# Batch 1's queries: from 32 half-width transposes of the loaded tile to 16 full ones of a copy repacked by GpSimd

## The chip, the cores and the metric

The kernel runs on one core of one Trainium2 chip. The metric is the device time of one execution in microseconds. The kernel before took 283.73 us, the median of six runs from 283.51 to 283.94.

## The reference

The program is a linear attention followed by a two-layer perceptron. `q`, `k` and `v` have shape 8 batches x 8 heads x 576 rows x 64.

```python
kv  = einsum('bhsd,bhse->bhde', k, v)      # 64 x 64 for each batch and head
out = einsum('bhsd,bhde->bhse', q, kv)
out = out / sqrt(mean(out * out, -1) + 1e-6) * g_norm
x   = out.transpose(0, 2, 1, 3).reshape(4608, 512)
h   = x @ w_in                             # 512 -> 2048
g   = where(h > 0, h, exp(min(h, 0)) - 1)
return g @ w_out                           # 2048 -> 512
```

The products run in bf16 with fp32 sums.

## The kernel before, in words

The 4608 rows are worked in nine tiles T. Tiles 0 to 7 are rows 0 to 511 of each batch (four groups j of 128 rows, `J = 4`, `G = 512`); tile 8 gathers the remaining 64 rows of every batch. Each tile passes through these stages:

1. the kv product of a batch (`kv_single`, L174): 64x64 matmuls of k and v into the PSUM buffer `at`, which ScalarE copies to `kv_sb` (L352);
2. the queries are turned, so that the 64 head dimensions lie on partitions (two heads to 128 partitions), into the tile `qT`;
3. the scores (L373 for tile 1, L201 later), then squares, sums over heads, reciprocal root and row scale, and a transpose into `xT`;
4. the first product `mm1` (L467), the elu (L479 to L498), and the second product `mm2` (L514), whose result ScalarE copies out (L527).

The order on every engine is written out by hand: the program runs under a manual schedule, each engine takes its instructions in the order in which the code issues them, and pieces of the attention of tile T + 1 are placed between the matmuls of tile T. `mm2_quarter(0, j, i)` is four matmuls of 128x512: row group j and weight slabs 4i to 4i+3 of tile 0's second product. The first eight pieces of that product are where the change is: quarter 0 for j = 0 to 3, then quarter 1 for j = 0 to 3.

Three ways of turning queries exist. Tile 0 has its own at the start. Tile 1, which the change touches, uses TensorE: `q_t` calls `q_t_single` (L185) for each of four head pairs, into a tile from the pool `ps_at`, which has one buffer of two PSUM banks. This tile is called `at` in the profile; kv products and some scores use the same one buffer. Two ScalarE copies (L249, L250) then move it to `qT`. Tiles from 2 on are repacked on GpSimd (`unpack_q`, four copies at L150) and turned by a transposing DMA (L256).

GpSimd's queue (POOL) holds nearly all loads, which also cast from fp32 to bf16. At most eight of them are under way: a load waits until the one eight places ahead of it has landed. For the stretch around the change the order is: k and v of batch 1, a small copy of batch 0's kv (L770), the weight slabs of `w_out` 10 to 12, 12 to 14 and 14 to 16 (L142), then q, k and v of batch 2. The queries of batch 1 were issued before, at 13.67 and 15.07 us, one transfer for each half of the heads, and lie in the tile `q_pk` as 128 rows x head x j x 64.

The code that sets the order around the change, before it:

```python
    load_w_out(10, 12)
    load_w_out(12, 14)
    ...
    for j in range(J):
        mm2_quarter(0, j, 0)
        if j == 2:
            at["q"]()
    for j in range(J):
        mm2_quarter(0, j, 1)
        if j == 1:
            at["kvu0"]()
        if j == 2:
            at["seu0"](scores)
```

`at["q"]` is `q_t` of tile 1, `at["kvu0"]` the kv product of its first half of head pairs, `at["seu0"]` the scores of that half.

Of the kernel before, what the change touches and what calls it, by code (L numbers as in the profile page):

```python
# [16 lines left out]
def kernel(  # L17
# [13 lines left out]
    nc = tc.nc  # L31
    P = 128
# [5 lines left out]
    J = 4  # L38
# [18 lines left out]
    ident = const.tile([P, P], BF16, name="ident")  # L57
# [13 lines left out]
    raw, bf = {}, {}  # L71
# [52 lines left out]
    def after(ap):  # L124
        nc.gpsimd.tensor_copy(out=gate, in_=ap)  # L125

    def unpack_q(b, eng):
        t = raw.pop(("q", b))
        bf["q", b] = qkvp.tile([P, J, H, D], BF16, name="q_bf", tag="q")
        for j in range(J):  # L130
            if j == J - 1:
                after(bf["v", b][0:1, 0, 0, 0:1])
            copy_on(eng, bf["q", b][:, j], t[:, :, j])

# [5 lines left out]
    def load_w_out(f0, f1):  # L140
        fs = slice(f0, f1)
        nc.gpsimd.dma_start(  # L142
            out=w_out_sb[:, fs, :], in_=moe_w_out.rearrange("(c p) f -> p c f", p=P)[:, fs, :]
        )

    def copy_on(eng, out_, in_):
        if eng is nc.scalar:
            nc.scalar.copy(out_, in_)
        else:
            eng.tensor_copy(out=out_, in_=in_)  # L150
# [13 lines left out]
    def at_tile(dtype):  # L164
        full = ps_at.tile([P, 1024], FP32, name="at", tag="at")
        return full if dtype == FP32 else full.bitcast(BF16)
# [12 lines left out]
                        stop=(j == RK - 1),  # L179
                    )  # L180

    def q_t_single(q_pk, qt_ps, r, p):
        for j in range(J):
            for l in range(2):
                nc.tensor.transpose(  # L185
                    qt_ps[l * 64 : l * 64 + 64, r, j * P : j * P + P],
                    q_pk[:, 2 * p + l, j, :],
                    ident,
                )

    def se_mm(T, h, qT, banks):

# [47 lines left out]
    def attention(T):  # L240
        st = {}

        def q_t():
            qt_ps = at_tile(BF16).rearrange("p (r t) -> p r t", r=NPAIR)
            qT = attp.tile([P, NPAIR, G], BF16, name="qT", tag="qT")
            st["qT"] = lambda p, j: qT[:, p, j * P : j * P + P]
            for p in range(NPAIR):
                q_t_single(raw["q", T], qt_ps, p, p)
            nc.scalar.copy(qT[:, 0:2, :], qt_ps[:, 0:2, :])  # L249
            nc.scalar.copy(qT[:, 2:4, :], qt_ps[:, 2:4, :])  # L250

# [152 lines left out]
        def x_u(u, eng):  # L404
# [21 lines left out]
            return turn  # L426

        pieces = {"kv": kv_all, "q": q_t, "qd": q_dma, "se": se}
        pieces["landed"] = lambda: after(st["at"])
        for h in range(2):  # L430
# [78 lines left out]
    def mm2(T, j, f0, f1, hold=False):  # L509

        if f0 == 0 and (T, j) not in o_ps:
            o_ps[T, j] = ps_m2.tile([P, DM], FP32, name="o_ps", tag="mm2")
        for f in range(f0, f1):
            nc.tensor.matmul(  # L514
                o_ps[T, j],
                lhsT=gT[T][:, f, j * P : j * P + P],
                rhs=w_out_sb[:, f, :],
                start=(f == 0),
                stop=(f == FC - 1),
            )  # L520
        if f1 == FC and not hold:
            mm2_out(T, j)
# [8 lines left out]
    def mm2_quarter(T, j, i):  # L531
        mm2(T, j, 4 * i, 4 * i + 4)
# [18 lines left out]
    V, A, Q = nc.vector, nc.scalar, nc.gpsimd  # L551
# [72 lines left out]
    def turned(n):  # L624
        return bank(n).bitcast(BF16).rearrange("p (r t) -> p r t", r=2)
# [3 lines left out]
    qt_ps = turned(3)  # L629
# [137 lines left out]
    at, ahead = attention(1), attention(2)  # L767
# [3 lines left out]
        out=kv_sb[:, 0].rearrange("p (s u) e -> p u s e", s=2), in_=kv0  # L771
    )
    load_w_out(10, 12)
    load_w_out(12, 14)
    load_w_out(14, FC)
    fetch_packed_q(2)
# [6 lines left out]
    scores = ps_m1.tile([P, 2, G], FP32, name="se_ps", tag="mm1")  # L783
    for j in range(J):
        mm2_quarter(0, j, 0)
        if j == 2:
            at["q"]()
    for j in range(J):
        mm2_quarter(0, j, 1)
        if j == 1:  # L790
            at["kvu0"]()
        if j == 2:
            at["seu0"](scores)
            at["sq0"]()
            at["sum0"]()
# [9 lines left out]
    for j in range(J):  # L805
        mm2(0, j, 10, 12)
        if j == 1:
            at["inv1"]()
            at["xu0"](scores[:, 0, :])
    at["mulu1"]()  # L810
    unpack_q(2, Q)
    ahead["qd"]()
    for j in range(J):
# [8 lines left out]
    def fetch(b):  # L822
        if b < B:
            fetch_packed_q(b)
            packed_kv(b)
            for name in "kv":
                fetch_packed_kv(name, b)
            unpack_q(b, Q)
        else:
            fetch_q(B)  # L830
            cast_q(B, Q)
# [46 lines left out]
    at, ahead = ahead, attention(3)  # L878
# [22 lines left out]
    for T in range(2, NT):  # L901
        at = ahead if T + 1 < NT else None
# [62 lines left out]
```

## Time and profile before

| | |
|---|---|
| median of 6 runs | 283.73 us (283.51 to 283.94) |
| the profiled execution | 283.93 us, span 282.2 us |
| TensorE busy | 273.2 us, 97% of the span |
| VectorE, ScalarE, GpSimd busy | 159.7, 153.7, 55.9 us |
| granted TensorE clock | 1.00 |
| L185, the 32 transposes | one after the other from 31.36 us, 1.01 us in all |
| L150, GpSimd's copies for tiles 2 to 7 | 24, 609 ns median |

The profile names instructions by line, engine, operation and tile. PE is TensorE's matmul, PEld its weight load, ACT ScalarE, DVE VectorE, POOL GpSimd. Times in the timeline are microseconds from the span's start, and in brackets stands how long the engine was idle before an instruction and what ended that. The span is shorter than the execution's own time by 1.7 us, which lies around it. Some matmul records are missing from the trace, so that counts there can be one or two short (x11 for 12).

### The profile page before, as it was taken

To read this page: it belongs to the slowest core of one execution; us is meant where nothing else is said; L and a number is where in the kernel's file an instruction comes from. 1 tells how busy PE (TensorE), PEld (TensorE's weight loads), DVE (VectorE), ACT (ScalarE), POOL (GpSimd) and SP (SyncE) were. 2 spreads that over 40 slices of the span, in tenths; PEclk is the share of its full clock that TensorE was granted. 3 is DMA by queue.
4 is the path that set the end of the run, shared out by engine and by line. 5 is a ranking of instruction groups with operands and counts; after the bars stand their busy time and mean duration, and the time that the engine had idled before them with its cause. 6 is when DMAs were issued, how large, how long until landed. Compare 5 with 4: busy or idle time off the path is not lost.

```text
span 282.2 us, 5133 instructions
## 1 busy us (share of the span) xinstructions
PE 273.2 (97%) x2104; PEld 129.1 (46%) x2134; DVE 159.7 (57%) x232; ACT 153.7 (54%) x221; POOL 55.9 (20%) x98
## 2 busy tenths in 40 slices
PE   7899999999999999999999999999999999999994
PEld 3434454445444444444444444444444444444444
DVE  2549443878388647843693468445854586444400
ACT  2769546666487438533863377237923692333311
POOL 7944422143421241005100421012000000000000
PEclk9999999999999999999999999999999999999999
DMA  7999999697796695358935795455236123010122
GB/s 196 199 200 202 208 201 191 145 196 136 173 194 102 153 177 139 74 149 118 203 76 146 95 216 69 127 115 150 53 95 77 77 38 112 0 77 0 74 76 74
DMA packets 57579, 35.98 MB, mean 128 GB/s; under 512 B 32852, under 2 KB 55124, under 8 KB 57556
## 3 DMA queue, kind: packets, MB, share of 16 engines
q0 software_dynamic: 21808, 17.30, 40.6%
q1 hardware_dynamic: 35348, 17.83, 25.3%
q10 hardware_dynamic: 400, 0.52, 0.5%
q8 instruction: 16, 0.26, 0.4%
q14 instruction: 7, 0.06, 0.1%
HBM read 36.70 MB, written 9.44 MB: 164 GB/s over the span
## 4 chain that ended last, share of the span: by engine, by line
PE 90%; DMA 5%; ACT 1%; issue 1%; DVE 1%; POOL 1%; POOLq 0%
PE h_ps L467 40%; PE o_ps L514 38%; PE o_ps L924 5%; DMA w_in_sb<-in_moe_w_in_dram 3%; DMA k_pk<-in_k_dram 2%; PE at L174 2%; PE at L467 1%; PE at L201 1%; PE bank L684 1%; POOL w_in_sb L136 1%; PE se_ps L201 1%; DVE xs L229 0%; DVE ss L218 0%; ACT elu_e L479 0%; PE at L185 0%
## 5 line engine op out<-in xcount | busy, mean ns | idle before, releaser
L467 PE MATMUL h_ps<-xT,w_in_sb 128*128 128x512 bf16 x532 | 125.5, 379 | 0.2
L514 PE MATMUL o_ps<-w_out_sb,gT 128*128 128x512 bf16 x488 | 118.1, 379 | 1.5 <-issue 0.5
L479 ACT ACTIVATE elu_e<-h_ps 128x1024 bf16<-128x1024 f32 (+1 forms) x71 | 69.9, 995 | 80.8 <-PE h_ps L467 78.5
L467 PEld LDWEIGHTS <-w_in_sb 128*128 128x128 bf16 x552 | 52.5, 98 | 63.2 <-DVE xT L333 1.7
L514 PEld LDWEIGHTS <-gT 128*128 128x128 bf16 x512 | 49.4, 98 | 58.4
L490 DVE TENSOR_SCALAR elu_e<-elu_e 128x1024 bf16<-128x1024 bf16 (+1 forms) x75 | 32.1, 428 | 73.8 <-ACT elu_e L479 73.8
L498 DVE TENSOR_TENSOR gT<-elu_e,h_ps 128x1024 bf16<-128x1024 bf16 (+1 forms) x51 | 60.1, 1179 | 5.3
L527 ACT COPY o_sb<-o_ps 128x512 f32<-128x512 f32 x32 | 18.6, 585 | 15.6 <-PE o_ps L514 15.6
L218 DVE TENSOR_REDUCE ss<-sq 128x16 f32<-128x1024 bf16 x16 | 19.4, 1219 | 11.2 <-ACT sq L213 10.5
L485 ACT ACTIVATE elu_h<-h_ps 128x1024 bf16<-128x1024 f32 (+1 forms) x20 | 19.6, 991 | 0.0
L150 POOL COPY q_bf<-q_pk 128x512 bf16<-128x512 bf16 x24 | 14.4, 629 | 22.9 <-DMA q_pk<-in_q_dram 22.9
L498 DVE TENSOR_TENSOR gT<-elu_e,elu_h 128x1024 bf16<-128x1024 bf16 x20 | 13.8, 692 | 2.6 <-ACT elu_h L485 1.2
L924 PE MATMUL o_ps<-w_out_sb,gT 128*128 128x512 bf16 (+1 forms) x79 | 14.0, 336 | 0.1
L125 POOL COPY gate<-qT 1x1 bf16<-1x1 bf16 x6 | 1.1, 180 | 61.9 <-DMA qT<-q_bf 61.9
L104 POOL DMA_DIRECT2D q_pk<-in_q_dram x14 | 10.5, 757 | 4.3 <-issue 1.5
L229 DVE TENSOR_TENSOR xs<-at,ss 128x512 bf16<-128x512 f32 x16 | 10.2, 681 | 1.2 <-ACT ss L225 1.2
L924 PEld LDWEIGHTS <-gT 128*128 128x128 bf16 x80 | 7.7, 98 | 6.4 <-DVE gT L498 0.4
L213 ACT ACTIVATE sq<-at 128x1024 bf16<-128x1024 f32 x9 | 9.4, 1044 | 1.6 <-PE at L201 1.0
L118 POOL DMA_DIRECT2D k_pk<-in_k_dram x12 | 8.3, 695 | 2.9 <-DMA w_in_sb<-in_moe_w_in_dram 1.2
L118 POOL DMA_DIRECT2D v_pk<-in_v_dram x12 | 8.3, 688 | 3.3 <-DMA w_out_sb<-in_moe_w_out_dram 1.8
L174 PEld LDWEIGHTS <-k_pk 64*64 64x64 bf16 x576 | 6.4, 107 | 4.5 <-issue 4.4
L932 ACT COPY o_last<-o_ps 128x512 f32<-128x512 f32 (+1 forms) x5 | 2.5, 500 | 10.8 <-PE o_ps L924 10.8
(79 smaller groups left out, 138.8 us busy)
## 6 DMA issues: line engine op xcount, KB each, us to landing
out_dram<-o_sb SPq DMA_DIRECT2D x16, 512.0 KB, 3.3
q_pk<-in_q_dram POOLq DMA_DIRECT2D x14, 256.0 KB, 5.4
k_pk<-in_k_dram POOLq DMA_DIRECT2D x6, 576.0 KB, 8.0
v_pk<-in_v_dram POOLq DMA_DIRECT2D x6, 576.0 KB, 10.8
w_in_sb<-in_moe_w_in_dram POOLq DMA_DIRECT2D x5, 256.0 KB, 8.4
st_q<-in_q_dram SPq DMA_DIRECT2D x2, 512.0 KB, 4.7
w_out_sb<-in_moe_w_out_dram POOLq DMA_DIRECT2D x2, 512.0 KB, 13.5
w_out_sb<-in_moe_w_out_dram POOLq DMA_DIRECT2D x4, 256.0 KB, 12.1
```

The costliest lines, as they stand in the source:

```text
L118: nc.gpsimd.dma_start(out=raw[name, b].rearrange("p h j d -> p h (j d)")[:, hs], in_=in_[:, hs])
L150: eng.tensor_copy(out=out_, in_=in_)
L174: nc.tensor.matmul(kv_ps[l * 64 : l * 64 + 64, s, u * 64 : u * 64 + 64], lhsT=bf["k", T][rows, j, 2 * u + l, :], rhs=bf["v", T][rows, j, 2 ...
L218: nc.vector.reduce_sum(out=ss, in_=sq.rearrange("p c (h e) -> p (c h) e", h=H), axis=AX.X)
L467: nc.tensor.matmul(h_ps[a][:, cs], lhsT=w_in_sb[:, c, f * P : f * P + P], rhs=x(c, cs), start=(c == 0), stop=(c == KC - 1),)
L479: nc.scalar.activation(e[:, lo:hi, :], ps, AF.Exp)
L485: nc.scalar.activation(h[:, lo:hi, :], ps, AF.Relu)
L490: nc.vector.tensor_scalar(out=e[:, lo:hi, :], in0=e[:, lo:hi, :], scalar1=1.0, scalar2=1.0, op0=ALU.min, op1=ALU.subtract,)
L498: nc.vector.tensor_tensor(out=gT[T][:, 2 * i + lo : 2 * i + hi, :], in0=e[:, lo:hi, :], in1=h, op=ALU.add if relu else ALU.max,)
L514: nc.tensor.matmul(o_ps[T, j], lhsT=gT[T][:, f, j * P : j * P + P], rhs=w_out_sb[:, f, :], start=(f == 0), stop=(f == FC - 1),)
L527: nc.scalar.copy(o_sb[T][:, j % 2, :], o_ps.pop((T, j)))
L924: nc.tensor.matmul(ps, lhsT=gT[B][:, f, j * P : j * P + P], rhs=w_out_sb[:, f, cols], start=(f == 0), stop=(f == FC - 1),)
```

## The change

Batch 1 gets the repacking that the later batches have. `unpack_q` gets a flag: for the later batches a tiny gating copy stands ahead of the last of its four copies, and for batch 1 it is left out. Its four GpSimd copies, each 128x512 bf16, are issued between the loads of slabs 10 to 12 and 12 to 14; they write the tile `q_bf` as 128 rows x j x head x 64. There two heads lie side by side, so that `q_t_single` takes 128 columns at once: 16 transposes of 128x128 in place of 32 of 128x64 in two halves. The call of `at["q"]` moves from behind quarter 0, j = 2, to behind quarter 1, j = 0: eight matmuls later. The two ScalarE copies, the buffer `at` and all that follows keep their order.

```diff
-    def unpack_q(b, eng):
+    def unpack_q(b, eng, gated=True):
         t = raw.pop(("q", b))
         bf["q", b] = qkvp.tile([P, J, H, D], BF16, name="q_bf", tag="q")
         for j in range(J):
-            if j == J - 1:
+            if gated and j == J - 1:
                 after(bf["v", b][0:1, 0, 0, 0:1])
             copy_on(eng, bf["q", b][:, j], t[:, :, j])
...
-    def q_t_single(q_pk, qt_ps, r, p):
+    def q_t_single(qb, qt_ps, p):
         for j in range(J):
-            for l in range(2):
-                nc.tensor.transpose(
-                    qt_ps[l * 64 : l * 64 + 64, r, j * P : j * P + P],
-                    q_pk[:, 2 * p + l, j, :],
-                    ident,
-                )
+            nc.tensor.transpose(
+                qt_ps[:, p, j * P : j * P + P],
+                qb[:, j, 2 * p : 2 * p + 2, :].rearrange("p h d -> p (h d)"),
+                ident,
+            )
...
-                q_t_single(raw["q", T], qt_ps, p, p)
+                q_t_single(bf["q", T], qt_ps, p)
...
     load_w_out(10, 12)
+    unpack_q(1, Q, gated=False)
     load_w_out(12, 14)
...
     for j in range(J):
         mm2_quarter(0, j, 0)
-        if j == 2:
-            at["q"]()
     for j in range(J):
         mm2_quarter(0, j, 1)
+        if j == 0:
+            at["q"]()
         if j == 1:
             at["kvu0"]()
```

## The prediction

> **What bounds the kernel now.** I read the page first, then the waits of TensorE, then the chain of waits in order of time, and last the timeline of all engines around the edited place. The page's first part settles the engine:
>
> ```profile
> PE 273.2 (97%) x2104; PEld 129.1 (46%) x2134; DVE 159.7 (57%) x232; ACT 153.7 (54%) x221; POOL 55.9 (20%) x98
> ```
>
> TensorE (PE) works 273.2 of 282.2 us. What lies off TensorE is free as long as TensorE does not wait for it. The waits of TensorE, all five that are listed:
>
> ```profile
> PE bank L603 <- DVE zeros L579: 1.5, 1, 1.5
> PE kv_ps L174 <- DMA v_pk<-in_v_dram: 0.7, 2, 0.5
> PE o_ps L514 <- issue: 0.5, 3, 0.2
> PE bank L684 <- DMA w_in_sb<-in_moe_w_in_dram: 0.5, 1, 0.5
> PE bank L666 <- ACT sq L663: 0.4, 2, 0.2
> ```
>
> Four of them belong to the start (lines 603, 684, 666 and the first kv product). After that only 0.5 us of "issue" is listed, and no wait for another engine or a DMA. So after about 20 us TensorE is a gapless queue: time taken off it is gained, time put into it as a stall is lost, and there is no later wait that could swallow a delay. Now the edited place in the chain (start us, us, what):
>
> ```profile
> 31.36 1.01 PE at L185 x32
> 32.38 0.16 issue
> 32.54 2.54 PE o_ps L514 x11
> 35.07 0.41 PE at L174 x36
> ...
> 41.31 0.45 PE se_ps L413 x8
> ```
>
> and the same place in the timeline of all engines (start us, us, engine, instruction, in brackets the idle time before it and who ended it):
>
> ```profile
> 29.02 0.70 POOL L142 DMA_DIRECT2D w_out_sb<-in_moe_w_out_dram x1 [0.61 <-DMA q_pk<-in_q_dram]
> ...
> 31.29 1.08 PE L185 MATMUL at<-ident,q_pk 128*64 128x128 bf16 x32
> 31.51 0.71 POOL L142 DMA_DIRECT2D w_out_sb<-in_moe_w_out_dram x1 [1.80 <-DMA w_out_sb<-in_moe_w_out_dram]
> ...
> 32.42 1.01 ACT L249 COPY qT<-at 128x1024 bf16<-128x1024 bf16 x1 [1.67 <-PE at L185]
> ...
> 32.96 0.74 POOL L104 DMA_DIRECT2D q_pk<-in_q_dram x1 [0.74 <-DMA k_pk<-in_k_dram]
> 33.33 1.02 ACT L250 COPY qT<-at 128x1024 bf16<-128x1024 bf16 x1
> ...
> 35.00 0.48 PE L174 MATMUL at<-v_pk,k_pk 64*64 64x64 bf16 x36
> ```
>
> What to see: the pool `at` has one buffer. The transposes of L185 fill it, ScalarE (ACT) empties it in two copies that start 0.91 us apart and end at 33.33 + 1.02 = 34.35, and the next user of the same buffer is the kv product of L174, at 35.00. The slack between "emptied" and "wanted again" is **0.65 us**. It is made by the 12 big matmuls that stand between L185 and L174 (11 of them recorded), 2.5 us.
>
> **What the Trainium skill says.** (1) "TensorE: Matmul & The Clock Gate", section "Wait — 56ns, not 53.3ns?": 55.6 ns from start to start for 128 columns and 215.7 ns for 512. The trace agrees: eight full 128x128 transposes of L413 take 0.45 us, 56 ns each; eight matmuls of L467 take 1.73 us, 216 ns each. (2) "TensorEngine Tiling (Array Packing)", "Column Tiling" and "Key Properties": with a stationary side of 64 columns two tiles work side by side, and a change of tiling mode drains the engine. The trace agrees: 32 half transposes take 1.01 us, 31.6 ns each, little more than half of 56, and behind them the chain has 0.16 us of "issue"; behind the full transposes of L413 it has none. (3) "GPSIMD Engine Reference", "Key points": GpSimd shares its SBUF interfaces with VectorE. In the trace 24 copies of L150 took 602 to 880 ns, median 609; so contention is there, but seldom. (4) The first page again, "What's actually happening": TensorE's clock is cut after an idle window of about 3.4 us. The trace has the clock at full speed throughout, and nothing in it shows so long a gap in mid-run; the stall I expect is about a third of that.
>
> **The change, part by part.**
>
> *TensorE work.* Removed: 32 half transposes, 1.01 us, and probably the 0.16 us drain behind them. Added: 16 full ones, 16 x 56 ns = 0.90 us. Sum: -0.11 to -0.27 us; I take -0.27, since no drain follows L413. That is 0.1% of the kernel, so the headline edit is almost nothing by itself: half-width transposes were already running in pairs.
>
> *GpSimd queue.* Added behind the weight load of slabs 10 to 12 (issued at 27.70): four copies. The first needs the second half of q_pk, whose arrival releases the queue at 29.02 in the timeline. Four at the 0.576 us pitch of the later groups (three in 1.73 us) end at 29.02 + 2.3 = 31.3; at the slowest copy seen, 880 ns, at 32.5. Passed by them in this queue: the load of slabs 12 to 14 moves from 29.02 to about 31.4, that of 14 to 16 from 31.51 to about 32.1; the two q_pk fetches and k_pk, v_pk of batch 2 keep their times, because the first of them waits until 32.96 for an older k transfer anyway. The moved loads cost nothing, I estimate: a transfer issued in this stretch lands 12.1 us later (29.02 gives 41.1), the transfers before it land some 1.3 us apart in issue order (38.5, 39.8, 41.1 from issue plus time to landing), so its bytes start to move only near 39.8, long after 31.4. If that cover were gone it would land at 31.4 + 12.1 = 43.5, against a first use near 42.6 + 1 us of the shift below: no wait to speak of even then.
>
> *VectorE.* Nothing is added; its elu operations at 28.97 to 31.5 could be slowed by the copies, but what they write (the last slabs of gT) is read at 44 us.
>
> *The move of the transposes.* They go eight matmuls later: 8 x 216 ns = 1.73, from 31.36 to **33.09**. Their input is there (31.3; 32.5 at worst). They end at 33.09 + 0.90 = 33.99. ScalarE's first copy started 0.05 us after all of L185 had ended (32.37, then 32.42), though the engine had been idle for 1.67 us and half of the transposes was done at about 31.9; so it waits for the whole set. In the changed program too only the first copy carries a wait for TensorE. Hence first copy 34.04, second 34.95, end 35.97.
>
> *The new wait.* TensorE, after the transposes, has only the four matmuls of one block, 0.86 us, before the kv product: it is there at 33.99 + 0.86 = 34.85, and `at` is free at 35.97. With 0.08 us from the end of a ScalarE copy to the weight load that it releases (L352 ends 39.85, L373's load starts 39.93), the product starts at **36.05** instead of 35.07 or 35.00: a stall of 1.2 us. Net of the 0.27 us saved and the rest of the order unchanged, everything from the product on is later by 36.05 - 35.00 = **1.05 us**. Behind the stalled product queue all later matmuls, since TensorE keeps their order. ScalarE's kv copy, the scores, squares, sums and row scales hang on the product and shift along with it; their distances to TensorE's later work stay as they were. Transfers get 1.05 us more slack.
>
> *Sum.* +1.05 us on the profiled execution: 283.93 becomes 284.98 (span 282.2 to 283.25). That execution lies 0.20 us above the median of the six runs, 283.73; so I predict **284.8 us**.
>
> *Bounds of the unknown.* Below: if the first copy could start at half of the transposes (33.59), the second would start at 34.50, end at 35.52, and the shift be 0.6. Another 0.1 could be swallowed at 40.34, where four matmuls took 0.97 us instead of 0.86, perhaps waiting for slabs 10 to 12. Above: +0.16 if a drain remains somewhere before the copies, +0.2 for a slower release: about 1.4. I take 1.05, because every term has a row.
>
> **The rivals.**
>
> - *No stall counts* (not slower): ScalarE's drain is overlapped or the shift is absorbed, and only the 0.27 us of TensorE work remains: 283.73 - 0.27 = 283.46 us. Place: the first matmul of the kv product. It decides if `at` is empty by 34.85. For it: ScalarE is idle just before (1.67 us at 32.42), so it copies at once. Against: both copies together need 1.93 us after the last transpose, and TensorE has 0.86 us of work there.
> - *Half-early drain*: the copies chase the transposes, shift 0.5 to 0.6, 284.3 us, at the edge of what counts. Against: the start at 32.42 after 1.67 us idle.
> - *GpSimd late* (slower still): the copies slip behind 33.09, by a late q_pk or contention with VectorE. It decides once four copies take over 4.1 us from 29.02, 1.0 us each; the slowest seen is 0.88. At 1.25 us each they end at 34.0: +0.9 more, 285.7 us.
> - *The full-width form is slower than I think*, drain included, at the price of separate 128-column matmuls: no, L413 shows 56 ns in this very kernel.
>
> **How the numbers follow.** Stall as computed, 84%; half-early 6%, GpSimd late 4%, no stall 6%. About 0.2% (0.57 us) is what a measurement of this kernel can tell from no change. Slower by more: 84 + 4 and a part of the half-early case: 0.88. Within: 0.09. Faster by more: 0.03, for what I don't see, since the TensorE work removed is worth less than 0.57 us. The range, 284.2 to 285.3 us, takes the main case with its bounds (0.6 to 1.4 above 283.73 gives 284.3 to 285.1) and a little for the median's own scatter.
>
> **What would show it.** In the profile after: the 16 transposes at about 33.1, 0.9 us long, with no wait for GpSimd; four copies on POOL from 29.0 to 31.3; the load of slabs 12 to 14 at 31.4; the two ScalarE copies at 34.0 and 34.95; and a new row in TensorE's waits, the kv product behind the copy into qT, about 1.2 us, once. I am wrong if that row is missing, if TensorE waits for q_bf, or if a wait for w_out appears near 42 to 45 us.

## The result, and the profile after

The changed kernel took **284.61 us**, the median of 19 runs (284.26 to 285.33), beside 283.8 us for the kernel before on the same chips. The ratio is 1.003 with a 95% interval of 1.002 to 1.0039, so the change costs 0.6 to 1.1 us: slower, by a little. The prediction was 284.8, from 284.2 to 285.3.

The page of the profile after, TensorE's row:

```profile
PE 272.9 (96%) x2088; PEld 129.3 (46%) x2118; DVE 159.7 (56%) x232; ACT 153.8 (54%) x221; POOL 59.2 (21%) x102
```

TensorE works 0.3 us less than before, in 16 matmuls less, and the span is nevertheless longer, 283.5 us in place of 282.2. The four longest waits of TensorE (us in total, times, longest) say why:

```profile
PE bank L602 <- DVE zeros L578: 1.5, 1, 1.5
PE kv_ps L174 <- DMA v_pk<-in_v_dram: 1.2, 2, 1.0
PE at L174 <- ACT qT L249: 1.2, 1, 1.2
PE o_ps L513 <- issue: 0.5, 3, 0.2
```

The third row is new, and there is one of it: the kv product of batch 1 behind the second ScalarE copy. The second row, 1.2 in place of 0.7, lies in the first microseconds, which neither edit touches: the loads at the start fall a little differently in every execution. In this one the second product of tile 0 began at 28.92 us, before at 28.61. I therefore compare two distances in which that start cancels: **d**, from the first matmul of that product to the first one of batch 1's kv product, and **R**, from the same matmul to the end of the span.

The timeline of the changed kernel at the edited place (line numbers from 184 up to the edited calls near the end are one lower than before):

```profile
28.91 2.60 POOL L150 COPY q_bf<-q_pk 128x512 bf16<-128x512 bf16 x4 [0.39 <-DMA q_pk<-in_q_dram]
28.92 4.48 PE L513 MATMUL o_ps<-w_out_sb,gT 128*128 128x512 bf16 x19
...
30.42 0.62 DVE L489 TENSOR_SCALAR elu_e<-elu_e 128x1024 bf16<-128x1024 bf16 x1
31.14 0.91 DVE L497 TENSOR_TENSOR gT<-elu_e,elu_h 128x1024 bf16<-128x1024 bf16 x1
31.46 1.40 POOL L142 DMA_DIRECT2D w_out_sb<-in_moe_w_out_dram x2
...
33.24 1.06 PE L184 MATMUL at<-ident,q_bf 128*128 128x128 bf16 x16
...
34.33 1.01 ACT L248 COPY qT<-at 128x1024 bf16<-128x1024 bf16 x1 [3.27 <-PE at L184]
...
35.24 1.02 ACT L249 COPY qT<-at 128x1024 bf16<-128x1024 bf16 x1
36.06 0.74 POOL L118 DMA_DIRECT2D k_pk<-in_k_dram x1 [0.77 <-DMA w_out_sb<-in_moe_w_out_dram]
36.31 0.48 PE L174 MATMUL at<-v_pk,k_pk 64*64 64x64 bf16 x36 [1.15 <-ACT qT L249]
```

Read it from the bottom. The kv product sat idle for 1.15 us and started 0.05 us after the second copy into qT had ended (35.24 + 1.02 = 36.26). The first copy began 1.09 us after the first transpose, where before it was 1.13, but now only four matmuls, not twelve, lie between the transposes and the product. Before the change the product of batch 1 began at 35.00, and the second product of tile 0 here:

```profile
28.61 2.75 PE L514 MATMUL o_ps<-w_out_sb,gT 128*128 128x512 bf16 x12
```

So d is 36.31 - 28.92 = 7.39 us, before 35.00 - 28.61 = 6.39: **+1.00 us**. R is 283.5 - 28.92 = 254.6, before 282.2 - 28.61 = 253.6: **+1.0 us**. Nothing of the stall was won back later. The remaining 0.3 us by which the two spans differ is the start.

### The profile page after: what moved, and what is told of

It reads as the page before. It is cut to its first block, busy times and chain, and to the rows that moved or that the text cites. A ratio compares the mean times of both kernels' runs of the same rounds, so it can differ in the third digit from the quotient of the medians.

```text
span 283.5 us, 5104 instructions
## 1 busy us (share of the span) xinstructions
PE 272.9 (96%) x2088; PEld 129.3 (46%) x2118; DVE 159.7 (56%) x232; ACT 153.8 (54%) x221; POOL 59.2 (21%) x102
## 4 chain that ended last, share of the span: by engine, by line
PE 89%; DMA 5%; ACT 2%; issue 1%; DVE 1%; POOL 1%; POOLq 0%
PE h_ps L466 40%; PE o_ps L513 37%; PE o_ps L924 5%; DMA w_in_sb<-in_moe_w_in_dram 3%; DMA v_pk<-in_v_dram 2%; PE at L174 2%; PE at L466 1%; PE at L200 1%; PE bank L683 1%; PE se_ps L200 1%; DVE xs L228 0%; DVE ss L217 0%; ACT elu_e L478 0%; ACT qT L248 0%; ACT sq L212 0%
## 5 line engine op out<-in xcount | busy, mean ns | idle before, releaser
L150 POOL COPY q_bf<-q_pk 128x512 bf16<-128x512 bf16 x28 | 17.5, 658 | 22.2 <-DMA q_pk<-in_q_dram 22.2
L932 ACT COPY o_last<-o_ps 128x512 f32<-128x512 f32 (+1 forms) x5 | 2.5, 501 | 10.8 <-PE o_ps L924 10.8
```

## The experiments

My theory, "one buffer": the loss is the read-out of the one-buffer tile `at`, which the move brought too close to the next user of that buffer. The main rival, "repacking": GpSimd's copies, the loads that they push back, or the full-width form cost the time. All times are medians beside runs of the kernel before on the same chip; d, R and the stall are read from one profiled execution of each kernel.

| kernel | d, us | R, us | stall, us | median, us | ratio to before (95%) |
|---|---|---|---|---|---|
| before | 6.39 | 253.6 | none | 283.7 to 283.9 | |
| the change | 7.39 | 254.6 | 1.15 | 284.61 | 1.003 (1.002 to 1.0039) |
| e1_old_place | 6.17 | 253.3 | none | 283.58 | 0.9996 (0.9988 to 1.0005) |
| e2_move_only | 7.51 | 254.6 | 1.05 | 284.83 | 1.004 (1.0027 to 1.0052) |
| e3_half_way | 6.52 | 253.6 | 0.29 | 284.08 | 1.001 (1.0 to 1.002) |
| e4_later | 8.26 | 256.9 | 2.02 | 287.01 | 1.0107 (1.0087 to 1.0128) |
| e5_dve_drain | 6.79 | 254.3 | 0.56 | 284.63 | 1.0026 (1.0014 to 1.0038) |
| e6_copies_only | 6.40 | 253.5 | none | 283.89 | 1.0008 (0.9995 to 1.0022) |
| e7_filled | 8.25 | 255.4 | 0.50 beside 1.5 of filling | 285.32 | 1.0057 (1.0044 to 1.007) |
| e8_later_dve | 7.66 | 255.2 | 1.43 | 285.42 | 1.0057 (1.0043 to 1.007) |

### The repacking without the move: e1_old_place

```diff
     for j in range(J):
         mm2_quarter(0, j, 0)
+        if j == 2:
+            at["q"]()
     for j in range(J):
         mm2_quarter(0, j, 1)
-        if j == 0:
-            at["q"]()
```

> The changed program, but the transposes stay where they were before the change (behind quarter 0, j = 2). Measure beside the time: d, from the first matmul of tile 0's second product to the first one of the kv product (6.39 us before, 7.39 us after the change). Theory 'one buffer' (the stall is the read-out of the single buffer at, which the move put too close to the kv product): the copies into qT end about 0.5 us before the buffer is wanted again, no stall, d = 6.2 to 6.4 (at most 0.2 of waiting for GpSimd's last copy), time 0 to 0.25 us under before, about 283.6. Rival 'repacking' (GpSimd's copies, the moved loads or the full-width form carry the cost): the time stays near that of the change, some 284.6 to 284.8.

Its timeline around the transposes:

```profile
28.56 2.52 POOL L150 COPY q_bf<-q_pk 128x512 bf16<-128x512 bf16 x4 [0.38 <-DMA q_pk<-in_q_dram]
...
31.08 1.06 PE L184 MATMUL at<-ident,q_bf 128*128 128x128 bf16 x16
...
33.08 1.02 ACT L249 COPY qT<-at 128x1024 bf16<-128x1024 bf16 x1
...
34.66 0.48 PE L174 MATMUL at<-v_pk,k_pk 64*64 64x64 bf16 x36
```

The last copy on GpSimd ends at 31.08 and the transposes begin at 31.08, without a listed wait: just in time in this execution. The buffer is empty at 34.10, 0.56 us before it is wanted. d is 6.17, 0.22 us under before, and R about 0.3 under. So with the move taken back the loss is gone, and what the repacking is worth by itself shows in the profile: about a quarter of a microsecond. The timing (0.9988 to 1.0005) cannot tell this from nothing. No other version has a median below that of the kernel before beside it.

### The move without the repacking: e2_move_only

```diff
     for j in range(J):
         mm2_quarter(0, j, 0)
-        if j == 2:
-            at["q"]()
     for j in range(J):
         mm2_quarter(0, j, 1)
+        if j == 0:
+            at["q"]()
```

This is applied to the kernel before.

> The program before with one edit: the 32 half-width transposes of the loaded tile are issued eight matmuls later, where the change has its 16. No repacking. Theory 'one buffer': the whole loss is here, and a little more since the half-width form is 0.2 us slower: d = 7.5, stall 1.0 to 1.2 us, time about 1.1 us over before, 284.9. Rival 'repacking': no loss, 283.8.

The row in TensorE's waits comes with the move alone:

```profile
PE at L174 <- ACT qT L250: 1.1, 1, 1.1
```

d is 7.51 and the median 284.83: the whole loss, without an added copy on GpSimd. "Repacking" is out.

This run also shows what the half-width transposes cost, since all four matmuls behind them are recorded:

```profile
33.07 1.08 PE L185 MATMUL at<-ident,q_pk 128*64 128x128 bf16 x32
34.09 1.04 PE L514 MATMUL o_ps<-w_out_sb,gT 128*128 128x512 bf16 x4
```

The 20 matmuls of 216 ns from 28.66 on (19 recorded) reach to 32.98, so the block of transposes takes 34.09 - 32.98 = 1.11 us of TensorE. The full-width block of the change takes 34.13 - 33.24 = 0.89. The difference, 0.22, is what e1_old_place gained in d. From the first start to the last the two forms are nearly alike, 0.86 and 0.84 us (1.08 and 1.06 less the 0.22 us that one transpose lasts). The saving is nearly all idle time at the two ends of the half-width block, of which 0.09 us lies ahead of it (32.98 to 33.07).

### Half way, and later: e3_half_way and e4_later

The edits are like that of e1_old_place, with the call behind quarter 0, j = 3, and behind quarter 1, j = 1, ahead of the kv product.

> The changed program with the transposes four matmuls earlier than in the change (behind quarter 0, j = 3), so half way between the two places. Theory 'one buffer': the buffer is free 0.86 us earlier than in the change, d = 6.5, a stall of about 0.3 us, time 0.1 to 0.2 us over before, 283.9. A rival in which the stall does not go with the distance (a fixed cost of the new form) says 284.6 to 284.8.

> The changed program with the transposes four matmuls later still (behind quarter 1, j = 1, straight ahead of the kv product). Theory 'one buffer': nothing of the read-out is covered any more, stall 2.0 us, d = 8.25, time about 1.85 us over before, 285.6. Fixed-cost rival: 284.6 to 284.8.

The wait and the two ends of d, first e3_half_way, then e4_later:

```profile
PE at L174 <- ACT qT L249: 0.3, 1, 0.3
28.07 3.62 PE L513 MATMUL o_ps<-w_out_sb,gT 128*128 128x512 bf16 x15
...
34.59 0.48 PE L174 MATMUL at<-v_pk,k_pk 64*64 64x64 bf16 x36 [0.29 <-ACT qT L249]
```

```profile
PE at L174 <- ACT qT L249: 2.0, 1, 2.0
28.36 5.34 PE L513 MATMUL o_ps<-w_out_sb,gT 128*128 128x512 bf16 x23
...
36.62 0.48 PE L174 MATMUL at<-v_pk,k_pk 64*64 64x64 bf16 x36 [2.02 <-ACT qT L249]
```

From e3_half_way over the change to e4_later each step of four matmuls (0.86 us) lengthens d by 0.87, from 6.52 to 7.39 to 8.26. A fixed cost of the new form is excluded. The times of e3_half_way agree (1.001, 1.0 to 1.002). Those of e4_later do not: 287.0 where I expected 285.6, and R is 3.3 us over before where d explains 1.9. Its page has a dip in the row of the granted clock, and the table by stretches of time (PE, PEld, DVE, ACT, POOL busy us and instructions, then the clock, the DMA share and GB/s) shows where:

```profile
PEclk9999979999999999999999999999999999999999
```

```profile
35.00:37.00 2.00, 0.38 (x36) 0.36 (x35) 0.00 (x0) 1.56 (x2) 1.06 (x2) 1.00 1.21 205
37.00:39.00 2.00, 1.84 (x33) 0.95 (x23) 0.00 (x0) 0.62 (x2) 0.74 (x1) 0.74 1.24 209
39.00:41.00 2.00, 2.00 (x6) 0.70 (x5) 1.22 (x1) 0.71 (x2) 0.00 (x0) 0.50 1.28 199
41.00:43.00 2.00, 1.84 (x42) 0.83 (x41) 1.29 (x2) 0.75 (x3) 0.00 (x0) 0.90 1.44 197
```

After the gap TensorE ran at half clock for 3.41 us: stretches of 0.02 us put the fall at 37.98 and the rise at 41.39. What is missing from full clock in the last three rows is 2 x (0.26 + 0.50 + 0.10) = 1.7 us. Of the five executions four have a mean clock of 0.994 and took 286.73 to 287.17 us; the fifth had 1.000 and took 285.53, what the stall alone predicts.

### A faster read-out: e5_dve_drain

```diff
-            nc.scalar.copy(qT[:, 0:2, :], qt_ps[:, 0:2, :])
-            nc.scalar.copy(qT[:, 2:4, :], qt_ps[:, 2:4, :])
+            nc.vector.tensor_copy(out=qT[:, 0:2, :], in_=qt_ps[:, 0:2, :])
+            nc.vector.tensor_copy(out=qT[:, 2:4, :], in_=qt_ps[:, 2:4, :])
```

> The changed program, but both copies of the turned queries into qT run on VectorE, which has nothing to do from 32 to 39 us, instead of ScalarE. Theory 'one buffer': a VectorE pass over 128x1024 bf16 of PSUM takes 0.75 us in the profile (L422) against 1.01 on ScalarE, so the buffer is free about 0.5 us earlier, d = 6.9 (7.39 in the change, 6.39 before), the stall falls from 1.15 to about 0.65 us, time about 0.5 us over before, 284.3. If TensorE waited for something else there (landing of k or v, a drain), d would stay at 7.39 and the time at 284.7.

Its timeline:

```profile
33.39 0.69 DVE L248 COPY qT<-at 128x1024 bf16<-128x1024 bf16 x1 [2.01 <-PE at L184]
33.99 0.68 DVE L249 COPY qT<-at 128x1024 bf16<-128x1024 bf16 x1
34.77 0.48 PE L174 MATMUL at<-v_pk,k_pk 64*64 64x64 bf16 x36 [0.56 <-issue]
```

With the place unchanged and only the read-out faster, d falls by 0.60 to 6.79, and the product again starts 0.10 us after the second copy. The stall follows the read-out. (A version in which the product has a buffer of its own was not run.) The time follows less well: R is 0.7 over before, where d accounts for 0.4. One new row of 0.2 us, TensorE waiting for a gT of VectorE in the last tile, is part of that: VectorE begins this gT 0.45 us after its preceding operation has ended, 0.10 in the change. Why, stays open. The expected 284.3 lies within the interval (1.0014 to 1.0038 of 283.71 is 284.1 to 284.8), but the measured median does not separate this version from the change.

### GpSimd's part by itself: e6_copies_only

```diff
     load_w_out(10, 12)
+    unpack_q(1, Q, gated=False)
     load_w_out(12, 14)
```

In the kernel before, with the flag that `unpack_q` then needs; the copies' result is not read.

> The program before with GpSimd's four copies of batch 1's queries added at the place where the change has them; what they write is not read, TensorE goes on turning the loaded tile. The copies push the loads of w_out slabs 12 to 14 and 14 to 16 back as in the change. Theory 'one buffer': GpSimd's part is free, d = 6.39, no new wait, 283.8 as before, and slabs 12 to 14 land within 0.3 us of where they landed before. Rival 'repacking': part of the 0.8 us shows here, 284.2 or more.

d is 6.40, R 253.5, TensorE has no new wait. The ratio, 1.0008, does not exclude a few tenths (0.9995 to 1.0022); the profile shows none. The two elu operations of VectorE at the end of the copies took 0.71 and 0.91 us here, so the slowing comes with the added copies. The loads of slabs 12 to 14 and 14 to 16 went out together at 30.93 and landed after 10.0 us (the median of the two), where in the kernel before they took 12.1 and 10.8: they wait in the queue of transfers instead of on GpSimd.

### What the gap does to the clock: e7_filled and e8_later_dve

e7_filled is e4_later with filling in the gap, e8_later_dve is e4_later with the copies of e5_dve_drain.

```diff
             at["q"]()
+            for f in range(7):
+                nc.tensor.matmul(
+                    scores[:, 0, :],
+                    lhsT=gT[0][:, f, 0:P],
+                    rhs=w_out_sb[:, f, :],
+                    start=True,
+                    stop=True,
+                )
```

> The program of e4_later with seven extra 128x512 matmuls between the transposes and the kv product; what they write is overwritten by the scores. They fill the stall of 2.0 us with 1.5 us of work (7 x 216 ns) and so move nothing by themselves: the kv product still waits for the second copy. Theory 'the gap of 2 us cuts the clock' (e4_later showed half clock from about 37 to 41 us in its profile and a mean clock of 0.994 in four of five executions, while the fifth, at 1.000, took 285.53): the clock stays at 1.000, d = 8.25 as there, time 285.5. Rival 'the late place itself costs 3 us' (another wait behind it): 287.0 as in e4_later, whatever the gap is filled with.

> The program of e4_later (transposes straight ahead of the kv product) with both copies into qT on VectorE. The read-out takes 0.6 us less, as e5_dve_drain showed, so the stall is 1.4 us in place of 2.0, d = 7.65. Theory 'one buffer': 1.25 us over before, 285.0, if the clock holds. For the clock it shows a gap between the 1.15 us of the change (never cut) and the 2.0 us of e4_later (cut in four of five): a mean clock of 0.994 and some 286.5 us in part of the executions would say that 1.4 us is already enough.

The table by stretches of e7_filled, two stretches:

```profile
35.00:37.00 2.00, 1.50 (x42) 0.80 (x41) 0.00 (x0) 1.41 (x3) 0.90 (x2) 1.00 1.21 205
37.00:39.00 2.00, 2.00 (x25) 0.89 (x23) 0.00 (x0) 0.97 (x2) 0.58 (x1) 1.00 1.24 207
```

Seven matmuls whose result is not used make e4_later 1.7 us faster (285.32 against 287.01). The kv product starts at the same distance, d = 8.25, and the clock stays at full speed, with means of 0.998 to 1.000 in five executions. So some 1.5 to 1.7 us of e4_later's loss was the clock, and the gap was its cause. In e8_later_dve, with a gap of 1.43 us, none of five executions shows the drop (0.998 to 1.000). Its median, 285.42, is 0.4 over what I expected; like e5_dve_drain it has the 0.2 us wait for gT in the last tile, which stays open.

## Why the prediction was right

- **TensorE's work**, -0.27 us: right in kind, a little large: -0.22 in d of e1_old_place, about -0.3 in R. What was mis-sized is the 0.16 us of "issue". It stands where the first of the 12 matmuls behind the transposes has no record: the 11 that have one follow each other without a hole up to the kv product. By e2_move_only the half-width block costs 1.11 us in all, not 1.01 + 0.16 = 1.17. The predicted time does not rest on this term, since the product waits for the copies, and these follow the transposes.
- **GpSimd's copies**, 2.3 us for four: 2.60 in the change, 2.47 to 2.52 in other runs. They ended at 31.51 instead of 31.3, but the transposes came 1.7 us later still, so nothing waited.
- **The moved loads at no cost**: right. Slabs 12 to 14 went out at 31.46 instead of 29.02 and, by 9.5 us to landing, arrived at 41.0 instead of 41.1.
- **VectorE slowed at no cost**: right, and now with a number. Beside the copies, the second of them only in its first 0.37 us, the elu's two operations took 0.62 and 0.91 us; before, they took 0.42 and 0.69:

```profile
30.10 0.42 DVE L490 TENSOR_SCALAR elu_e<-elu_e 128x1024 bf16<-128x1024 bf16 x1
...
30.78 0.69 DVE L498 TENSOR_TENSOR gT<-elu_e,elu_h 128x1024 bf16<-128x1024 bf16 x1 [0.26 <-ACT elu_h L485]
```

The contention that "GPSIMD Engine Reference", "Key points", of the Trainium skill leads one to expect is there; the copies, too, took longer than the 2.3 us of later groups.

- **The copies wait for all transposes**: right, since d is as computed from it; the half-early rival would have given 0.6 or less in place of 1.00.
- **The new wait**, 1.2 us: 1.15. The shift, 1.05 us: 1.00 in d and in R; the 0.05 is the release, 0.05 us where I had 0.08, and the start of the copies.
- **Nothing absorbs it**: right, R grew by as much as d.
- **The clock holds**: right for this stall, which no execution of the change shows with a drop like e4_later's. But the reason that I gave was weaker than I thought. "TensorE: Matmul & The Clock Gate", "What's actually happening", gives an idle window of about 3.4 us, and I took the stall to be a third of the danger. e4_later lost its clock after a gap of 2.02 us in four of five executions; here the measurement decides. That 1.15 us was safe was found by running it, not by that argument.

The median came out at 284.61 and not at 284.8: 0.8 over before where the profile has 1.0. The difference is within the interval.

## What to carry to other kernels

Before a step that fills a one-buffer tile is moved, measure the time from "emptied" to "wanted again" in the timeline: the move is free up to about that slack (0.65 us here) and costs one for one beyond it (0.87 us of d for each further 0.86), however idle the engine that empties the tile is. Half-width transposes that already run in pairs leave little to gain from full width (0.22 us here): compare the time of the whole block, with the idle time at its ends, not the count of instructions. Where a stall of TensorE of 2 us cannot be avoided, filling it can be worth as much as shortening it: filled it took 285.32 us, shortened to 1.43 us 285.42, as it was 287.01.

## What the runs showed that I had not expected

A gap of 2.02 us in an otherwise dense stream of matmuls was enough to cut TensorE's clock in four of five executions (half clock for 3.41 us in the one with a trace), at a price of 1.5 to 1.7 us; gaps of 1.15 us (19 runs) and 1.43 us (5 runs) never did. Between 1.43 and 2.02 us the limit is not known.

It may also depend on when the gap falls. In the clock records of all ten traces every complete stretch at one clock is a whole number of times 3.413 us: in e4_later 30.72 us of full clock (9 times), 3.41 of half (once), then 245.76 of full (72 times); in the other nine 273.07 to 279.89 of full (80 to 82 times). So the clock seems to be decided in steps of 3.41 us, and the step before the half clock, 34.56 to 37.98, contains the whole gap (34.60 to 36.62). A gap split between two steps might pass, which would explain the one execution of five that escaped; no run tests this, and that execution has no trace.

VectorE read 128x1024 bf16 of PSUM in 0.69 us where ScalarE took 1.01.
